# Gate columns and gate rows of an adaLN transformer block: from TensorE to GpSimd, VectorE and DRAM

## The chip, the cores and the metric

One NeuronCore of a Trainium2 chip runs the whole kernel. The metric is the device time of one execution in microseconds, as a median of runs. The engines are called by the names of the profile: PE (TensorE matmuls), PEld (TensorE weight loads), DVE (VectorE), ACT (ScalarE), POOL (GpSimd) and SP (SyncE, whose queue issues most of the DMAs).

## The reference

The block has 2048 rows of D = 1024, 32 query heads of 128, 4 key/value heads, the last 512 cached positions, and an FFN of width 3584. All inputs and the output are bf16.

```python
mod = (_silu(c) @ w_mod).reshape(c.shape[0], 6, 1, -1)
sa, ca, ga, sb, cb, gb = (mod[:, 0].copy(), ..., mod[:, 5].copy())
h = _layernorm(x, axis=-1) * (1 + ca) + sa
x = x + ga * _A_ref(h, A_k_cache, A_v_cache, A_wq, A_wo)   # attention, with wo
h = _layernorm(x, axis=-1) * (1 + cb) + sb
x = x + gb * _B_ref(h, B_w_gate, B_w_up, B_w_down)         # silu(h wg) * (h wu), then wd
```

c has one row, so the six modulation vectors sa to gb are the same for all 2048 rows of x. The two gates, ga and gb, scale the outputs of the attention and of the FFN.

## The kernel before

The rows of x are worked in four chunks of 512. For the attention the program is one loop over i from 1 to 129, with i = 32 * chunk + head. Each pass emits, in this order, the query projection for head i + 3 (8 matmuls of 512 columns into PSUM bank QB, emptied by a DVE cast at L640), the scores of head i - 1 (4 matmuls of 512 columns, whose exps ACT takes at L757 in two pieces of two banks), the product with V for head i - 2 (16 matmuls of 129 columns, normalised by DVE with a reciprocal at L775 and a multiply at L778), and a DMA transpose of that head's output into `oT_all` (L781, SP's queue). In passes up to 8 the query projection runs in every second pass only. When the last head of a chunk is through, `oproj` multiplies the 32 heads by wo, 8 pieces of 32 matmuls, and `resid` (L797 and L799) multiplies each piece by a gate row and adds it to x. After the attention, each chunk runs 28 gate and up column blocks and then the down projection, which ends in the same `resid`.

All instructions are issued in program order on each engine. `T.op` (L55) sets a semaphore wait ahead of an instruction for each buffer that another stream still writes or reads, so an instruction that waits holds everything behind it on its engine or, for a DMA, on SP's queue.

Small work is put into the passes by hand. `bg` is a list of generators; `run_bg(1)` at the end of each pass lets the first of them take one step. `ln_task` is one of these: for each of four 128-row tiles one step of `bn_stats` (L415), one of `bn_stats` and `bn_aggr` with two POOL instructions for the reciprocal deviation (L420, L422), and one of the norm (L426) with a DMA transpose (L445); three empty steps and four steps of two `modulate` (L431) follow.

The modulation vectors come in three ways. sa and ca are made before the loop by matmuls with one moving column. The last three vectors (sb, cb, gb) are made one column at a time from transposed weights by a DVE operation with an accumulator (`mod_col`, L585), in passes 38 to 89; for this, `sc_row` holds silu(c) along the free dimension in all partitions. The attention gate ga is made in passes 7 and 9 to 12, by 64 matmuls that take 128x128 blocks of `wga` as weights and one column of `sc_bf` (silu(c), one column for each 128 rows of w_mod) as the moving operand:

```python
for k in {7: (0, 1, 2, 3), 9: (4,), 10: (5,), 11: (6,), 12: (7,)}.get(i, ()):
    mod_mm(wga[:, k, :], B_wga[k], k, GCOLS)
```

The result is a vector across partitions (`mod_bf[:, NE:NF]`). `resid` and `mod_col` need such vectors as rows that are equal in all partitions. `row_task` does this three times (silu(c) into `sc_row`, ga into `rowb[0]`, gb into `rowb[1]`): POOL multiplies the identity by each of 8 columns (`diag`, L600), TensorE multiplies an all-ones matrix by the 8 diagonals (128 moving columns each, into bank XB), and DVE casts two halves to bf16 (L608).

The region `OFF_OT` of the arena holds early weights first and `oT_all`, 1 KB for each head, from then on. `wga` lies where the wo slots 6 and 7 come in passes 20 and 23.

Of the kernel before, what the change touches and what calls it, by code (L numbers as in the profile page):

```python
# [130 lines left out]
def bass_adaLN_cond__sliding_block_cached__swiglu_ffn__prompt_kernel(  # L131
# [50 lines left out]
    c_row = S_("c_row", [DT, P], BF16)  # L182
    sc_bf = S_("sc_bf", [P, DT], BF16)
    mod_bf = S_("mod_bf", [P, NJ], BF16)
    c6 = S_("c6", [P, DT], F32)
    mcol = S_("mcol", [P, 3 * DT], F32)
    gain = [S_("gain%d" % i, [P, DT], BF16) for i in range(2)]
    gain_f = S_("gain_f", [P, DT], F32)
    nmean = S_("nmean", [P, 1], F32)
# [19 lines left out]


    OFF_H20 = 154 * KB
    B_ident = _Buf("ident"); B_ones = _Buf("ones"); B_zw = _Buf("zw")
    B_diag = [_Buf("diag%d" % i) for i in range(4)]
    ident = arena.at(OFF_H20, [P], BF16, [B_ident])
    ones_bf = arena.at(OFF_H20 + 256, [P], BF16, [B_ones])
    diag = [arena.at(OFF_H20 + 512 + 256 * i, [P], BF16, [B_diag[i]]) for i in range(4)]
    zwarm = arena.at(OFF_H20 + 2048, [512], BF16, [B_zw])

    def bank(b, n=512, off=0):
        return ps[:, b * 512 + off:b * 512 + off + n]  # L220
# [7 lines left out]
    def psap(off, dims):  # L228
        return bass.AP(tensor=ps_t, offset=off, ap=[[4096, P]] + dims)
# [1 line left out]
    PB = [_Buf("bank%d" % b) for b in range(8)]  # L231
    B_x = [_Buf("x%d" % t) for t in range(ST)]
    B_mh = _Buf("mhalf")
    B_cT = _Buf("cT"); B_sc = _Buf("sc"); B_late = [_Buf("late%d" % i) for i in range(4)]; B_c6 = _Buf("c6"); B_mcol = _Buf("mcol"); B_scr = _Buf("scr")
    B_mode = _Buf("mode"); B_modc = _Buf("modc"); B_bq = _Buf("bq"); B_gf = _Buf("gf")
    B_nm = _Buf("nmean"); B_acc = _Buf("acc"); B_acc0 = _Buf("acc0")
    B_g = [_Buf("g%d" % i) for i in range(2)]
# [20 lines left out]
    with nc.Block() as block:  # L258

        @block.gpsimd  # L260
        def _(g):
# [5 lines left out]
            def mm(out_ap, lhsT, rhs, start, stop, reads, bank_buf, skip=False):  # L267
                T.op(PE, lambda: TE.matmul(out_ap, lhsT, rhs, start=start, stop=stop, skip_group_check=skip),  # L268
                     reads=reads, writes=[bank_buf])
# [15 lines left out]
            def finish(gen):  # L285
                while gen in bg:
                    run_bg(1)
# [3 lines left out]
            T.op(POOL, lambda: g.affine_select(out=ident, in_=ident, compare_op=ALU.not_equal,  # L291
                                               fill=1.0, base=0, pattern=[[-1, P]], channel_multiplier=1),
                 reads=[B_ident], writes=[B_ident])
            T.op(POOL, lambda: g.memset(ones_bf, 1.0), writes=[B_ones])
            T.op(POOL, lambda: g.memset(mhalf[:, :], -0.5), writes=[B_mh])
            T.op(POOL, lambda: g.memset(zwarm, 0.0), writes=[B_zw])

# [258 lines left out]

            B_wga = [_Buf("wga%d" % k) for k in range(DT)]
            wga = arena.at(OFF_WO + 48 * KB, [DT, D], BF16, B_wga)
            GCOLS = [(j, j) for j in range(DT)]

            def load_wga(i):
                T.op(dq("q_wga%d" % i), lambda: SP.dma_start(
                    wga[:, i * HK:(i + 1) * HK, :],
# [27 lines left out]
                     reads=[B_mcol], writes=[cbuf])  # L591


            def row_task(dst, dbuf, src, sbuf):
                T.op(POOL, lambda: g.tensor_copy(c6[:, :], src), reads=[sbuf], writes=[B_c6])

                def diags(n):
                    for q in range(4):
                        col = 4 * n + q
                        T.op(POOL, lambda: g.tensor_scalar(diag[q], ident, c6[:, col:col + 1], None, op0=ALU.mult),  # L600
                             reads=[B_ident, B_c6], writes=[B_diag[q]])

                diags(0)
                yield
                for n in range(2):
                    for q in range(4):
                        mm(bank(XB, P, q * P), ones_bf, diag[q], q == 0, q == 3, [B_ones, B_diag[q]], PB[XB], skip=True)
                    T.op(DVE, lambda: V.tensor_copy(dst[:, n * 512:(n + 1) * 512], bank(XB)),  # L608
                         writes=[PB[XB], dbuf])
                    if n == 0:  # L610
                        diags(1)
                    yield


            LEAD = 3
            NQT = 5; NEX = 2; NOS = 4
# [129 lines left out]
            o_s = [arena.at(OFF_OS + i * 1 * KB, [TPC, P], BF16, [B_os[i]]) for i in range(NOS)]  # L746
            oT_all = arena.at(OFF_OT, [Hq, CH], BF16, B_oT)

            def scores(i):
                ch, h = divmod(i, Hq)  # L750
                gk = h // rep
                qs = q_slot(i)
                es = i % NEX
                for kt in range(KT):
                    mm(bank(SCB + kt), kT_sb[:, gk * KT + kt, :], qT_s[qs], True, True, [B_kT[gk], B_qT[qs]], PB[SCB + kt])
                for kp in range(KT // 2):
                    T.op(ACT, lambda: A.activation(ex_s[es][:, 2 * kp:2 * kp + 2, :], banks2(SCB + 2 * kp), AF.Exp, scale=att_scale),  # L757
                         writes=[PB[SCB + 2 * kp], PB[SCB + 2 * kp + 1], B_ex[es]])
# [69 lines left out]
            def add_ln2(ch):  # L828
                s = ch % 2
                if ch == 0:  # L830
                    finish(rows)
                    h2s[0] = arena.at(OFF_H20, [DT, CH], BF16, B_h2[0])
                ln2[ch] = ln_task(ch, h2s[s], B_h2[s], 1, 3 * DT, B_late[1])
                bg.append(ln2[ch])

            LOADX = {19: 2, 40: 3}
            LOADT = {Hq + 2 + (9 * n) // 4: n for n in range(NL)}
            LOADO = {5 + (21 * p) // 8: p for p in range(8)}
            for i in range(1, NA + 2):
                ch, h = divmod(i, Hq)  # L840
                if i % 4 == 1 and i > 5 or i == 4:
                    load_wq((i + 4) // 4 + 1)
                if 2 <= i < NQ0:
                    q_shifted(i)
                if i in (2, 3):
                    load_wga(i - 2)
                if i in LOADX:
                    load_x(LOADX[i])
                if i in LOADO:
                    load_wo(LOADO[i])  # L850
                for gk in {2: (1,), 3: (2,), 4: (3,)}.get(i, ()):
                    k_turn(gk, XB)
                    kd, ks = k_evac(gk, XB)
                    T.op(DVE, lambda: V.tensor_copy(kd, ks), writes=[PB[XB], B_kT[gk]])
                    if gk == Hkv - 1:
                        for b_ in B_hT[1]:
                            for kb in B_kn:
                                b_.absorb(kb)
                if i == 17:
                    bg.append(row_task(sc_row, B_scr, sc_bf[:, :], B_sc))  # L860
                if i == 5:
                    add_ln1(1)
                if h == 2 and 1 <= ch < NCH - 1:
                    add_ln1(ch + 1)
                if h == 2 and ch == NCH - 1:
                    add_ln2(0)
                if i + LEAD < NA:
                    if (i + LEAD) % Hq == 0:
                        finish(ln1[(i + LEAD) // Hq])
                    if i == 1:  # L870
                        scores(0)
                    if i in (1, 3, 5):
                        q_bias_mm(i + 1, i + 3, QB)
                    if i > NQ0:
                        qproj(i + LEAD)
                    elif i % 2 == 0:
                        qproj(NQ0 - 1 + i // 2)
                for k in {7: (0, 1, 2, 3), 9: (4,), 10: (5,), 11: (6,), 12: (7,)}.get(i, ()):
                    mod_mm(wga[:, k, :], B_wga[k], k, GCOLS)
                    if k == DT - 1:  # L880
                        T.op(DVE, lambda: V.tensor_copy(mod_bf[:, NE:NF], psap(XB * 512, [[2, DT]])), writes=[PB[XB], B_late[0]])
                        rows = row_task(rowb[0], B_row[0], mod_bf[:, NE:NF], B_late[0])
                        bg.insert(0, rows)
                if i - 4 in LOADT:
                    n = LOADT[i - 4]
                    mod_col(n)
                    g0, last = divmod(n, DT)
                    if last == DT - 1:
                        mod_take(g0, B_late[g0 + 1])
                        if g0 == 1:  # L890
                            mod_gain(1, B_late[2], B_g[1])
                        elif g0 == 2:
                            rows = row_task(rowb[1], B_row[1], mod_bf[:, 5 * DT:6 * DT], B_late[3])
                            bg.insert(0, rows)
                if i in LOADT:
                    load_mt(LOADT[i])
                n = i - (NA - LEAD)
                if 0 <= n <= 2:
                    oproj_mm(NCH - 1, 0, QB, 8 * n, 8 * n + 8)
                elif n >= 3:  # L900
                    oproj_mm(NCH - 1, 1, XB, 8 * (n - 3), 8 * (n - 3) + 8)
                if 1 <= i - 1 < NA:
                    scores(i - 1)
                if 0 <= i - 2 < NA:
                    pv(i - 2)
                    ch2, h2 = divmod(i - 2, Hq)
                    if h2 == Hq - 1 and ch2 < NCH - 1:
                        finish(rows)
                        oproj(ch2)
                run_bg(1)  # L910


            NWG = 3
# [146 lines left out]
```

## Time and profile before

| what | us |
|---|---|
| median of 3 runs | 1275.35 (1275.09 to 1275.66) |
| span of the profiled execution | 1273.8 |
| PE busy | 1267.0 |
| DVE busy | 479.6 |
| ACT busy | 341.5 |
| POOL busy | 42.0 |
| 256 exps at L757, each | 1.023 |
| 24 diagonal multiplies at L600, each | 0.616 |
| 24 `mod_col` at L585, each | 1.214 |

The page gives the profiled execution as the span from its first to its last instruction; the runs are timed from outside and stand 1.55 us above that. A row of the timeline gives the start in us from the span's start, the time taken, the engine, the line, the operation, its output and inputs with their shapes, how many instructions are merged into the row, and in brackets how long the engine had been idle and what it waited for. In a row of merged instructions, the time runs from the first start to the last end.

### The profile page before, as it was taken

To read this page: it belongs to the slowest core of one execution; us is meant where nothing else is said; L and a number is where in the kernel's file an instruction comes from. 1 tells how busy PE (TensorE), PEld (TensorE's weight loads), DVE (VectorE), ACT (ScalarE), POOL (GpSimd) and SP (SyncE) were. 2 spreads that over 40 slices of the span, in tenths; PEclk is the share of its full clock that TensorE was granted. 3 is DMA by queue.
4 is the path that set the end of the run, shared out by engine and by line. 5 is a ranking of instruction groups with operands and counts; after the bars stand their busy time and mean duration, and the time that the engine had idled before them with its cause. 6 is when DMAs were issued, how large, how long until landed. Compare 5 with 4: busy or idle time off the path is not lost.

```text
span 1273.8 us, 17943 instructions
## 1 busy us (share of the span) xinstructions
PE 1267.0 (99%) x7683; PEld 645.7 (51%) x7683; DVE 479.6 (38%) x897; ACT 341.5 (27%) x388; POOL 42.0 (3%) x102
## 2 busy tenths in 40 slices
PE   8999999999999999999999999999999999999999
PEld 5665545555455564455544444444444444444444
DVE  4655315764147652365322331233212331222222
ACT  4555304554025550155510111011100111011100
POOL 1020000000000010000000000000000000000000
PEclk9999999999999999999999999999999999999999
DMA  9999403876018641055253973056411644035200
GB/s 306 271 235 224 99 1 84 194 169 133 1 34 191 140 104 38 5 129 118 67 147 99 285 222 121 25 154 152 148 60 56 192 140 132 17 120 161 66 9 25
DMA packets 235854, 155.31 MB, mean 122 GB/s; under 512 B 129024, under 2 KB 222080, under 8 KB 235776
## 3 DMA queue, kind: packets, MB, share of 16 engines
q1 hardware_dynamic: 177520, 95.45, 30.7%
q10 hardware_dynamic: 58256, 58.73, 14.7%
q8 instruction: 60, 0.98, 0.3%
q14 instruction: 18, 0.15, 0.0%
HBM read 119.54 MB, written 4.19 MB: 97 GB/s over the span
## 4 chain that ended last, share of the span: by engine, by line
PE 99%; DMA 1%; DVE 0%; SPq 0%; ACT 0%; issue 0%
PE ps L268 98%; DMA arena<-in_A_wq_dram 1%; DVE arena L671 0%; SPq L331 0%; SPq L306 0%; PE ps L272 0%; ACT arena L757 0%; DVE arena L666 0%; DVE tmp L797 0%; DVE arena L799 0%; DVE bq L661 0%
## 5 line engine op out<-in xcount | busy, mean ns | idle before, releaser
L268 PE MATMUL ps<-arena 128*128 128x512 bf16 (+1 forms) x7378 | 1260.7, 334 | 4.0 <-POOL arena L408 2.2
L268 PEld LDWEIGHTS ps<-arena 128*128 128x128 bf16 x7378 | 635.6, 98 | 621.0 <-issue 3.9
L757 ACT ACTIVATE arena<-ps 128x1024 bf16<-128x1024 f32 x256 | 261.9, 1023 | 350.3 <-PE ps L268 338.4
L989 ACT ACTIVATE arena<-ps 128x512 bf16<-128x512 f32 x112 | 66.9, 597 | 506.4 <-PE ps L268 506.4
L990 DVE TENSOR_TENSOR arena<-ps,arena 128x512 bf16<-128x512 f32 x112 | 77.4, 691 | 276.6 <-PE ps L268 276.6
L797 DVE TENSOR_TENSOR tmp<-ps,rowb 128x512 f32<-128x512 f32 (+1 forms) x65 | 44.4, 683 | 318.8 <-PE ps L268 318.8
L640 DVE CAST arena<-ps 128x512 bf16<-128x512 f32 x120 | 82.9, 691 | 53.8 <-PE ps L268 53.8
L778 DVE TENSOR_TENSOR arena<-ps,rl 128x512 bf16<-128x512 f32 x128 | 88.5, 691 | 4.7 <-DVE rl L775 0.3
L775 DVE RECIPROCAL rl<-ps 128x4 f32<-128x4 f32 x128 | 23.3, 182 | 118.3 <-PE ps L268 118.3
L415 DVE BATCH_NORM_STATS2 st<-x_res 128x6 f32<-128x512 bf16 x62 | 42.3, 683 | 3.6 <-DMA x_res<-in_A_x_dram 3.5
L420 POOL TENSOR_SCALAR rstd<-mv 128x1 f32<-128x1 f32 x28 | 6.3, 226 | 888.2 <-DVE mv L419 888.2
L585 DVE SCALAR_TENSOR_TENSOR arena<-arena 128x1024 bf16<-128x1024 bf16 x24 | 29.1, 1214 | 0.0
L799 DVE TENSOR_TENSOR arena<-tmp,x_res 128x512 bf16<-128x512 f32 (+1 forms) x33 | 22.3, 675 | 1.1
L799 DVE TENSOR_TENSOR x_res<-tmp,x_res 128x512 bf16<-128x512 f32 x32 | 22.1, 692 | 1.1
L431 DVE TENSOR_SCALAR arena<-arena,gain,mod_bf 128x512 bf16<-128x512 bf16 x56 | 20.3, 404 | 0.0
L426 DVE TENSOR_SCALAR nsc<-x_res,mv,rstd 128x1024 bf16<-128x1024 bf16 x30 | 16.0, 533 | 0.0
L422 POOL TENSOR_TENSOR rstd<-rstd,mhalf 128x1 f32<-128x1 f32 x28 | 15.8, 564 | 2.3
L600 POOL TENSOR_SCALAR arena<-arena,c 128x128 bf16<-128x128 bf16 x24 | 14.4, 616 | 32.7 <-PE ps L268 32.4
L268 PEld LDWEIGHTS ps<-sc_bf,arena 128*128 128x128 bf16 x192 | 6.6, 96 | 2.3 <-DMA arena<-in_w_mod_dram 0.3
L268 PE MATMUL ps<-sc_bf,arena 128*128 128x1 bf16 x192 | 6.8, 163 | 0.0
L419 DVE BATCH_NORM_AGGREGATE mv<-st 128x2 f32<-128x12 f32 x28 | 5.8, 209 | 1.0
L653 DVE COPY arena<-ps 128x512 f32<-128x512 f32 x4 | 2.7, 688 | 8.3 <-PE ps L268 8.3
(53 smaller groups left out, 50.7 us busy)
## 6 DMA issues: line engine op xcount, KB each, us to landing
arena<-in_A_wq_dram SPq DMA_DIRECT2D x31, 1024.0 KB, 6.1
arena<-in_B_w_gate_dram ACTq DMA_DIRECT2D x28, 1024.0 KB, 5.4
arena<-in_B_w_up_dram ACTq DMA_DIRECT2D x28, 1024.0 KB, 8.1
arena<-in_A_wo_dram SPq DMA_DIRECT2D x8, 1024.0 KB, 6.4
arena<-in_B_w_down_dram SPq DMA_DIRECT2D x7, 1024.0 KB, 8.4
out_dram<-arena SPq DMA_DIRECT2D x15, 256.0 KB, 2.0
x_res<-in_A_x_dram SPq DMA_DIRECT2D x3, 1024.0 KB, 6.7
arena<-in_w_mod_dram SPq DMA_DIRECT2D x8, 256.0 KB, 6.3
```

The source lines that it names most:

```text
L268: T.op(PE, lambda: TE.matmul(out_ap, lhsT, rhs, start=start, stop=stop, skip_group_check=skip), reads=reads, writes=[bank_buf])
L415: T.op(DVE, lambda: V.bn_stats(st_[sl][:, hf * 6:hf * 6 + 6], x_res[:, t, hf * 512:hf * 512 + 512]), reads=[B_x[t]], writes=[B_st[sl]])
L431: T.op(DVE, lambda: V.tensor_scalar(dst[:, dt, :], dst[:, dt, :], gain[gi][:, dt:dt + 1], mod_bf[:, ccol + dt:ccol + dt + 1], op0=ALU.mult ...
L585: T.op(DVE, lambda: V.scalar_tensor_tensor(mt[n % 2], mt[n % 2], 1.0, sc_row, op0=ALU.mult, op1=ALU.mult, accum_out=mcol[:, n:n + 1]), rea ...
L640: T.op(DVE, lambda: V.tensor_copy(qT_s[qs], bank(b)), writes=[PB[b], B_qT[qs]])
L757: T.op(ACT, lambda: A.activation(ex_s[es][:, 2 * kp:2 * kp + 2, :], banks2(SCB + 2 * kp), AF.Exp, scale=att_scale), writes=[PB[SCB + 2 * k ...
L775: T.op(DVE, lambda: V.reciprocal(rl[r][:, :].rearrange("p (a b) -> p a b", a=2), psap(PVB * 512 + P, [[512, 2], [130, 2]])), writes=both + ...
L778: T.op(DVE, lambda: V.tensor_tensor(o_s[os_].rearrange("p (a b) d -> p a b d", a=2), psap(PVB * 512, [[512, 2], [130, 2], [1, P]]), rlb, A ...
L797: T.op(DVE, lambda: V.tensor_tensor(tmp[s][:, 0:n], bank(b, n), rowb[ri][:, c0:c0 + n], ALU.mult), reads=[B_row[ri]], writes=[PB[b], B_tmp ...
L799: T.op(DVE, lambda: V.tensor_tensor(dst[:, c0:c0 + n], tmp[s][:, 0:n], x_res[:, t, c0:c0 + n], ALU.add), reads=[B_tmp[s], B_x[t]], writes= ...
L989: T.op(ACT, lambda: A.activation(sg_s[ss], bank(gb), AF.Silu), writes=[PB[gb], B_sg[ss]])
L990: T.op(DVE, lambda: V.tensor_tensor(guT[:, ft, :], bank(ub), sg_s[ss], ALU.mult), reads=[B_sg[ss]], writes=[PB[ub], B_gu[ft]])
```

## The change

ga is no longer made by TensorE. `wga` now serves as it lies in memory, with the rows of w_mod across partitions. For each of the 8 groups of 128 rows, a group is multiplied by its column of `sc_bf` (one scalar for each partition) and summed into an fp32 accumulator `g_acc` of 128x1024: groups 0 to 3 by POOL in pieces of 512 columns (`gate_part`, passes 4 to 13), groups 4 to 7 by DVE in one instruction each (`gate_row`, passes 16 to 19). Then POOL splits `g_acc` into a bf16 part and the bf16 remainder (`gate_split`), two DMA transposes on SP's queue turn the parts (`gate_turn`, passes 23 and 24), and DVE sums each of them over the former partitions and adds the two sums (`gate_sum`, passes 26 and 27).

The three rows are no longer made by `row_task`. `row_put` writes a vector from across the partitions to a row in DRAM, and `row_get` reads that row back into all 128 partitions, both on SP's queue.

The new tiles lie in `OFF_OT` in the place of heads that are written later in the first chunk: `g_tmp` at heads 16 and 17, `g_part` at 24 to 27, `g_acc` and after it `g_turn` at 28 to 31.

```diff
-            T.op(POOL, lambda: g.memset(ones_bf, 1.0), writes=[B_ones])
...
-            def row_task(dst, dbuf, src, sbuf):
...
+            def row_put(r, src, sbuf):
+                T.op(Q_dr[r], lambda: SP.dma_start(d_rows[r:r + 1, :].rearrange("o (k p) -> p (o k)", p=P), src, allow_slow_non_contiguous=True),
+                     reads=[sbuf], writes=[B_dr[r]])
+
+            def row_get(r, dst, dbuf):
+                rep_ap = bass.AP(tensor=d_rows.tensor, offset=r * D, ap=[[0, P], [1, D]])
+                T.op(Q_rw[r], lambda: SP.dma_start(dst, rep_ap), reads=[B_dr[r]], writes=[dbuf])
...
+            def gate_part(n):
+                k, hf = divmod(n, 2)
+                a = g_acc[:, hf * 512:(hf + 1) * 512]
+                w = wga[:, k, hf * 512:(hf + 1) * 512]
+                if k == 0:
+                    T.op(POOL, lambda: g.tensor_scalar(a, w, sc_bf[:, k:k + 1], None, op0=ALU.mult),
+                         reads=[B_wga[k], B_sc], writes=[B_ga[hf]])
+                else:
+                    T.op(POOL, lambda: g.tensor_scalar(g_tmp, w, sc_bf[:, k:k + 1], None, op0=ALU.mult),
+                         reads=[B_wga[k], B_sc], writes=[B_gx])
+                    T.op(POOL, lambda: g.tensor_tensor(a, a, g_tmp, ALU.add), reads=[B_gx], writes=[B_ga[hf]])
...
+            def gate_row(k):
+                T.op(DVE, lambda: V.scalar_tensor_tensor(g_acc, wga[:, k, :], sc_bf[:, k:k + 1], g_acc, op0=ALU.mult, op1=ALU.add),
+                     reads=[B_wga[k], B_sc], writes=B_ga)
+
+            def gate_split():
+                T.op(POOL, lambda: g.tensor_copy(g_part[0], g_acc), reads=B_ga, writes=[B_gp[0]])
+                T.op(POOL, lambda: g.tensor_tensor(g_part[1], g_acc, g_part[0], ALU.subtract),
+                     reads=B_ga + [B_gp[0]], writes=[B_gp[1]])
+
+            def gate_turn(i):
...
+                T.op(Q_gt[i], lambda: SP.dma_start_transpose(g_turn[i], g_part[i]), reads=[B_gp[i]], writes=[B_gt[i]])
...
+            def gate_sum(i):
+                T.op(DVE, lambda: V.tensor_reduce(gsum[:, i * DT:(i + 1) * DT], g_turn[i], mybir.AxisListType.X, ALU.add),
+                     reads=[B_gt[i]], writes=[B_gsum])
+                if i == 1:
+                    T.op(DVE, lambda: V.tensor_tensor(gcol[:, :], gsum[:, 0:DT], gsum[:, DT:2 * DT], ALU.add),
+                         reads=[B_gsum], writes=[B_gcol])
...
+            GATEP = {4: (0, 1), 5: (2,), 7: (3,), 8: (4,), 10: (5,), 11: (6,), 13: (7,)}
+            GATER = {16 + n: NGP + n for n in range(DT - NGP)}
+            GATET = {23: 0, 24: 1}
+            GATES = {26: 0, 27: 1}
+            t2 = Hq + 6 + (9 * (NL - 1)) // 4
+            PUTT = {22: (0, sc_bf[:, :], B_sc), 29: (1, gcol[:, :], B_gcol), t2 + 2: (2, mod_bf[:, 5 * DT:6 * DT], B_late[3])}
+            GETT = {25: (0, sc_row, B_scr), 31: (1, rowb[0][:, :], B_row[0]), t2 + 4: (2, rowb[1][:, :], B_row[1])}
...
-                if i == 17:
-                    bg.append(row_task(sc_row, B_scr, sc_bf[:, :], B_sc))
+                if i in GATET:
+                    gate_turn(GATET[i])
+                if i in GATES:
+                    gate_sum(GATES[i])
+                if i in GATER:
+                    gate_row(GATER[i])
+                if i in PUTT:
+                    row_put(*PUTT[i])
+                if i in GETT:
+                    row_get(*GETT[i])
...
-                for k in {7: (0, 1, 2, 3), 9: (4,), 10: (5,), 11: (6,), 12: (7,)}.get(i, ()):
-                    mod_mm(wga[:, k, :], B_wga[k], k, GCOLS)
-                    if k == DT - 1:
-                        T.op(DVE, lambda: V.tensor_copy(mod_bf[:, NE:NF], psap(XB * 512, [[2, DT]])), writes=[PB[XB], B_late[0]])
-                        rows = row_task(rowb[0], B_row[0], mod_bf[:, NE:NF], B_late[0])
-                        bg.insert(0, rows)
...
                 run_bg(1)
+                for n in GATEP.get(i, ()):
+                    gate_part(n)
+                if i == max(GATER):
+                    gate_split()
```

NGP is 4, DT is 8, NL is 24, so t2 is 89. The code before and after these lines stays as it is.

More of the change, by code (lines that the diff above doesn't have):

```diff
@@ L184, in bass_adaLN_cond__sliding_block_cached__swiglu_ffn__prompt_kernel @@
     mod_bf = S_("mod_bf", [P, NJ], BF16)
-    c6 = S_("c6", [P, DT], F32)
     mcol = S_("mcol", [P, 3 * DT], F32)
+    gsum = S_("gsum", [P, 2 * DT], F32)
+    gcol = S_("gcol", [P, DT], BF16)
     gain = [S_("gain%d" % i, [P, DT], BF16) for i in range(2)]
@@ L211, in bass_adaLN_cond__sliding_block_cached__swiglu_ffn__prompt_kernel @@
     OFF_H20 = 154 * KB
-    B_ident = _Buf("ident"); B_ones = _Buf("ones"); B_zw = _Buf("zw")
-    B_diag = [_Buf("diag%d" % i) for i in range(4)]
+    B_ident = _Buf("ident"); B_zw = _Buf("zw")
+    B_gcol = _Buf("gcol")
+    B_dr = [_Buf("dr%d" % i) for i in range(3)]
     ident = arena.at(OFF_H20, [P], BF16, [B_ident])
-    ones_bf = arena.at(OFF_H20 + 256, [P], BF16, [B_ones])
-    diag = [arena.at(OFF_H20 + 512 + 256 * i, [P], BF16, [B_diag[i]]) for i in range(4)]
+    d_rows = nc.dram_tensor("mod_rows", [3, D], BF16, kind="Internal").ap()
     zwarm = arena.at(OFF_H20 + 2048, [512], BF16, [B_zw])
@@ L233, in bass_adaLN_cond__sliding_block_cached__swiglu_ffn__prompt_kernel @@
     B_mh = _Buf("mhalf")
-    B_cT = _Buf("cT"); B_sc = _Buf("sc"); B_late = [_Buf("late%d" % i) for i in range(4)]; B_c6 = _Buf("c6"); B_mcol = _Buf("mcol"); B_scr = _Buf("scr")
+    B_cT = _Buf("cT"); B_sc = _Buf("sc"); B_late = [_Buf("late%d" % i) for i in range(4)]; B_gsum = _Buf("gsum"); B_mcol = _Buf("mcol"); B_scr = _Buf("scr")
     B_mode = _Buf("mode"); B_modc = _Buf("modc"); B_bq = _Buf("bq"); B_gf = _Buf("gf")
@@ L558, in _ @@
             wga = arena.at(OFF_WO + 48 * KB, [DT, D], BF16, B_wga)
-            GCOLS = [(j, j) for j in range(DT)]
             def load_wga(i):
@@ L591, in mod_take @@
                      reads=[B_mcol], writes=[cbuf])
-            def row_task(dst, dbuf, src, sbuf):
[L595 to L612, printed above, removed]
+            Q_dr = [dq("q_dr%d" % i) for i in range(3)]
+            Q_rw = [dq("q_rw%d" % i) for i in range(3)]
+            Q_gt = [dq("q_gt%d" % i) for i in range(2)]
+            def row_put(r, src, sbuf):
[4 more added lines that the diff above has]
+                T.op(Q_rw[r], lambda: SP.dma_start(dst, rep_ap), reads=[B_dr[r]], writes=[dbuf])
             LEAD = 3
@@ L747, in _ @@
             oT_all = arena.at(OFF_OT, [Hq, CH], BF16, B_oT)
+            NGP = 4
+            B_ga = [_Buf("ga%d" % i) for i in range(2)]
+            B_gx = _Buf("gx")
+            B_gp = [_Buf("gp%d" % i) for i in range(2)]
+            B_gt = [_Buf("gt%d" % i) for i in range(2)]
+            g_acc = arena.at(OFF_OT + 28 * KB, [D], F32, B_ga)
+            g_tmp = arena.at(OFF_OT + 16 * KB, [512], F32, [B_gx])
+            g_part = [arena.at(OFF_OT + (24 + 2 * i) * KB, [D], BF16, [B_gp[i]]) for i in range(2)]
@@ new lines, in _ @@
+            g_turn = [arena.at(OFF_OT + (28 + 2 * i) * KB, [DT, P], BF16, [B_gt[i]]) for i in range(2)]
+            def gate_part(n):
[9 more added lines that the diff above has]
+                    T.op(POOL, lambda: g.tensor_tensor(a, a, g_tmp, ALU.add), reads=[B_gx], writes=[B_ga[hf]])
+                if n == 2 * NGP - 1:
+                    for h in (16, 17):
+                        B_oT[h].absorb(B_gx)
@@ new lines, in gate_turn @@
+            def gate_turn(i):
+                for b_ in B_ga:
+                    B_gt[i].absorb(b_)
+                T.op(Q_gt[i], lambda: SP.dma_start_transpose(g_turn[i], g_part[i]), reads=[B_gp[i]], writes=[B_gt[i]])
+                for h in (24 + 2 * i, 25 + 2 * i):
+                    B_oT[h].absorb(B_gp[i])
+            def gate_sum(i):
[4 more added lines that the diff above has]
+                         reads=[B_gsum], writes=[B_gcol])
+                    for h in range(28, Hq):
+                        for b_ in B_gt:
+                            B_oT[h].absorb(b_)
@@ L830, in add_ln2 @@
                 if ch == 0:
-                    finish(rows)
                     h2s[0] = arena.at(OFF_H20, [DT, CH], BF16, B_h2[0])
@@ L891, in _ @@
                             mod_gain(1, B_late[2], B_g[1])
-                        elif g0 == 2:
-                            rows = row_task(rowb[1], B_row[1], mod_bf[:, 5 * DT:6 * DT], B_late[3])
-                            bg.insert(0, rows)
                 if i in LOADT:
@@ L907, in _ @@
                     if h2 == Hq - 1 and ch2 < NCH - 1:
-                        finish(rows)
                         oproj(ch2)
                 run_bg(1)
+                for n in GATEP.get(i, ()):
+                    gate_part(n)
+                if i == max(GATER):
+                    gate_split()
             NWG = 3
```

## The prediction

> **What bounds the kernel now.** I read the page's busy shares and the chain that ended last, then the granted clock, then the DVE timeline as a ruler of the attention loop.
>
> ```profile
> PE 1267.0 (99%) x7683; PEld 645.7 (51%) x7683; DVE 479.6 (38%) x897; ACT 341.5 (27%) x388; POOL 42.0 (3%) x102
> PEclk9999999999999999999999999999999999999999
> PE 99%; DMA 1%; DVE 0%; SPq 0%; ACT 0%; issue 0%
> ```
>
> TensorE is busy for 1267.0 of 1273.8 us, at the full clock (mean 1.000), and the chain is TensorE work. So a matmul taken out is worth its own time, and any other engine costs something only where it makes TensorE wait. The ruler is the reciprocal on L775, once in each loop pass, 0.20 us after the last pv matmul of the pass:
>
> ```profile
> 53.96 0.18 DVE L775 RECIPROCAL rl<-ps 128x4 f32<-128x4 f32 x1 [1.08 <-PE ps L268]
> 57.66 0.18 DVE L775 RECIPROCAL rl<-ps 128x4 f32<-128x4 f32 x1 [1.28 <-PE ps L268]
> ...
> 68.75 0.18 DVE L775 RECIPROCAL rl<-ps 128x4 f32<-128x4 f32 x1 [1.21 <-PE ps L268]
> 72.24 0.18 DVE L775 RECIPROCAL rl<-ps 128x4 f32<-128x4 f32 x1 [1.08 <-PE ps L268]
> 75.96 0.18 DVE L775 RECIPROCAL rl<-ps 128x4 f32<-128x4 f32 x1 [1.08 <-PE ps L268]
> ```
>
> 72.24 less 68.75 is the bare pass (3.497 with more digits; 35.87 belongs to pass i=2, so 53.96 to i=8, 72.24 to i=13). A pass with 8 gate-column matmuls takes 3.70 (57.66 less 53.96), one with 4 row matmuls 3.72 (75.96 less 72.24).
>
> **What is taken from TensorE.** Passes 9 to 12 lose 8 gate matmuls each: 4 x 0.20 = 0.80 us. The three row tasks lose two groups of four 128-column matmuls each: 6 x 0.224 = 1.34 us. The 32 gate matmuls of pass 7 are another matter, because ACT is late there:
>
> ```profile
> 47.69 0.94 PE L268 MATMUL ps<-sc_bf,arena 128*128 128x1 bf16 x32
> ...
> 48.50 1.70 PE L268 MATMUL ps<-arena 128*128 128x512 bf16 x16
> ...
> 48.74 1.33 PEld L268 LDWEIGHTS ps<-arena 128*128 128x128 bf16 x15 [0.15 <-ACT arena L757]
> ```
>
> Without them the scores start at 47.69 instead of 48.50. But their third matmul needs PSUM that the running pair of exps (46.55, 2.14 long) frees at 48.69; it then starts at 48.74 instead of 48.93 (48.50 + 2 x 0.2155). I count 0.17 us, the floor, rather than 0.81, the ceiling, because TensorE already meets ACT there. Sum: 0.80 + 1.34 + 0.17 = 2.31 us.
>
> The removed DVE casts (6 of 0.68 us), the diagonals on POOL and the memset of the ones save nothing: no TensorE wait names them, and the start waits for the c row (PEld 0.84 us behind its DMA).
>
> **GpSimd's half.** Two pieces of one instruction, six of two, on 128x512. The one-operand multiply is not in the trace at this size. Below it stands the 128x512 memset (0.52 us), above it four times the 128x128 multiply (4 x 0.616 = 2.46); by the slope from a 128x1 (0.226) to a 128x128 it is 0.226 + 511 x 0.00307 = 1.80, which I take, being the same operation. The fp32 add has only a 128x1 power (0.56) as a row: 0.56 to 3.6 (twice the multiply), taken at 1.8. The weights land by 29.4 + 7.8 = 37.2 us. Pieces 0 to 2 (four instructions, 7.2 us) end at 44.4; the layernorm step behind them on POOL gets its input at 49.65. Pieces 3 and 4 (7.2) run from 50.7 to 57.9; the next step is due at 59.5. Pieces 5 and 6 run from 60.4 to 67.6, due about 69. If the add costs 3.6, pieces 3 and 4 end at 61.5 and the rstd is 0.8 us late for the norm, which DVE's slack below covers.
>
> DVE and GpSimd may also hold each other up. The trace has one meeting of a GpSimd run with a fast DVE operation:
>
> ```profile
> 72.44 2.34 POOL L600 TENSOR_SCALAR arena<-arena,c 128x128 bf16<-128x128 bf16 x4 [2.15 <-PE ps L268]
> ...
> 93.15 2.61 POOL L600 TENSOR_SCALAR arena<-arena,c 128x128 bf16<-128x128 bf16 x4
> ...
> 94.50 0.54 DVE L426 TENSOR_SCALAR nsc<-x_res,mv,rstd 128x1024 bf16<-128x1024 bf16 x1
> ```
>
> GpSimd's four took 0.27 us more than where DVE read PSUM; the norm took its usual 0.54 and began on time. So DVE won, at no cost. The operations exposed are two shifts (passes 4 and 5), three norms (7, 10, 13) and the first modulates against the split. From above, each is held for a whole 1.8 us instruction; a norm may slip about 1.25 us before TensorE notices (0.37 idle ahead of the cast, 0.9 between cast and the next use of its bank), so three norms cost up to 3 x 0.55 = 1.6 us. The lower end is nothing; a gain is excluded, since no instruction gets shorter by company. I take 0.2, near the row.
>
> The Trainium skill, SBUF — State Buffer, section "Who interferes with whom", speaks against this change: the port pair that the two engines share is an exclusive lock, held for a whole instruction, and whoever starts second is fully blocked. By it DVE would lose whenever GpSimd is first; the one meeting in this trace does not show that, and it alone decides my 0.2. By the rule the sum would end near 1.6 worse.
>
> **DVE's half.** Four gate_row operations, passes 16 to 19, each ahead of the cast that empties the q projection's bank. Nearest row: L585, the same form on 128x1024, 1.214 us, its successor 1.14 behind its start; fp32 operands are not in the trace, from 0.69 (512 fp32 columns) to 2.4 (twice it), taken at 1.21. Pass 16 is the tight one, as its gate_row follows bn_stats and bn_aggr:
>
> ```profile
> 79.69 0.18 DVE L775 RECIPROCAL rl<-ps 128x4 f32<-128x4 f32 x1 [1.08 <-PE ps L268]
> ...
> 81.23 0.21 DVE L419 BATCH_NORM_AGGREGATE mv<-st 128x2 f32<-128x12 f32 x1
> 81.41 0.69 DVE L640 CAST arena<-ps 128x512 bf16<-128x512 f32 x1
> 83.18 0.18 DVE L775 RECIPROCAL rl<-ps 128x4 f32<-128x4 f32 x1 [1.08 <-PE ps L268]
> ```
>
> The cast moves from 81.41 to 82.55 and ends at 83.24, seen by TensorE at 83.29 (0.05 of latency, as behind the exp); it wants the bank at 82.98. Loss 0.31 us (nothing at 0.69, 1.5 at 2.4). Behind a norm (pass 17) the cast ends 0.16 before its bank is due, behind nothing earlier still: no loss in 17 to 19. The two reductions (passes 26, 27; no row, taken as 1.21 too) follow empty steps, likewise free.
>
> **SP's queue.** Two transposes like the layernorm's (issue 1.26, landing 3.6, at most 7.7). The first is issued at 106.9, behind the last wo load, and is needed at 115.5 (pass 26); the second at 109.8, needed at 119.0. At worst both are 0.9 us early. The split feeding them starts at 92.2 and takes 3.6 to 11, so it is done by 103. The wo load of pass 20 now waits for gate_row, done at 92.2; SP reaches it at 98.3. Each of the six row DMAs costs an issue of about 0.53; SP has over 0.4 us spare in each pass.
>
> The puts are the open point: each writes 1,024 runs of 2 bytes to DRAM, which no row shows. A wq load is also 1,024 runs:
>
> ```profile
> arena<-in_A_wq_dram SPq DMA_DIRECT2D x31, 1024.0 KB, 6.1
> ...
> out_dram<-arena SPq DMA_DIRECT2D x1, 128.0 KB, 1.7
> ```
>
> Between 1.6 (the 64 KB output) and 11.3 us (the slowest wq load), I take 6, being nearest in runs. The gate's put leaves at 128 behind a wq load and its get stands in SP's queue at 134.8; the get waits, and behind it the transposes of heads 29 to 31, but TensorE needs those (and the row) only at about 150. Counting back the get's issue, three transposes and 2.9 of landing (7.5 us together), the put may take 14.4 us before TensorE waits. For pass 22's put the room to its get is 11 us, and more behind it. The third row is first read in the down projection, after 645 us. Cost 0, also at 11.3.
>
> The Trainium skill, VectorE: DVE Perf Modes, section "The three transpose paths", warns that a strided plain copy is 19 times slower than a DMA transpose. By its 1.309 us for 128x128, a put of a sixteenth as many elements would be about 1.6 us (an estimate): this too stays covered.
>
> **Sum.** -2.31 + 0.31 + 0.2 = -1.8 us. The profiled span of 1273.8 becomes 1272.0; the median of the runs, 1275.35, lies 1.55 above the span, which I carry over: 1273.5 us. A measurement of this kernel tells about 0.2%, 2.55 us, from no change, so the forecast lies inside that band.
>
> **Rivals.**
> - Faster, 1272.4: pass 7 returns its full 0.81 and neither 0.31 nor 0.2 is lost (-2.95). For it: DVE is only 38% busy. Against it: the ACT wait at 48.74 and the back-to-back DVE at 81.4.
> - Slower, the put: it decides above 14.4 us, and from there each us of landing is one us of time. At 19.3 us it eats 2.3 and 2.55 more; at 25 it gives 1275.35 - 1.8 + 10.6 = 1284. For it: 2-byte runs are far from any row, and DMA is over 90% busy to 127 us. Against it: 256-byte transposes land in 2.9 us.
> - DVE held by GpSimd, or GpSimd slower than 2.6 us an instruction (10.5 us from 50.7 to the rstd's last useful start, for four), so that norms wait for rstd: three norms 1.6, a modulate behind a long split up to 3 more, 1275 to 1278. For it: GpSimd is busy through most of passes 4 to 14. Against it: the meeting at 94.5.
> - The change does nothing for TensorE: excluded by the ruler for all but pass 7.
>
> **How the numbers follow.** Forecast 0.57, faster 0.14, the put 0.12, DVE held 0.17. Two thirds of the last end beyond the band, so slower is 0.12 + 0.11 = 0.23, the same 0.57 + 0.06 = 0.63, faster 0.14. The range runs from 1272.2 (the faster rival with rounding) to 1278.0 (the top of the held case); it leaves out the put and little else. The forecast's own range is 1272.4 to 1275.0.
>
> **What would show it.** Right: passes 9 to 15 and the three former row passes at 3.497; pass 7 only 0.1 to 0.2 shorter; one pass near 16 about 0.3 longer; no SP wait on a put beyond a few us. Wrong: TensorE waits that name L640's bank in passes 5 to 14 (DVE held), a late first oproj near 143 us (the put), reductions waiting for the transposes, or GpSimd instructions well over 2.6 us.

## The result: 2.3% slower, and the profile after

The changed kernel takes 1304.84 us (median of 5 runs, 1302.57 to 1307.3) against 1275.66 for the kernel before beside it (5 runs): a ratio of 1.0228, 95% interval 1.0217 to 1.0239. The forecast was 1273.5, so it was missed by about 31 us. The profiled execution took 1305.02 us, its span is 1303.1, 29.3 more than before.

The head of the page after, the clock by slices, and the chain that ended last:

```profile
span 1303.1 us, 17621 instructions
...
PE 1263.0 (97%) x7454; PEld 644.0 (49%) x7595; DVE 485.1 (37%) x897; ACT 341.7 (26%) x388; POOL 51.0 (4%) x90
...
PEclk9998889999999999999999999999999999999999
...
PE 92%; DMA 5%; DVE 1%; issue 1%; SPq 1%; ACT 0%
```

TensorE has 88 matmuls fewer, the 64 of the gate columns and the 24 of the rows, as the count of its weight loads shows (7595 for 7683; the trace lacks some records of matmuls, so their own count says less). But its share fell from 99 to 97% and the clock dips in three slices, from 98 to 195 us. DMA, 1% of the chain before, now has 5%. The ruler (the reciprocal, now on L815) says where. Each row gives what the passes took beyond the same passes of before:

| stretch | more or less, us |
| --- | --- |
| to the first ruler tick (pass 2) | -0.28 |
| passes 3 to 15 | -1.41 |
| pass 17, whose bank is freed by pass 16's cast, behind a gate_row | +0.36 |
| passes 26 (18.269 for 3.496) and 27 (6.626 for 3.496) | +17.90 |
| passes 29, 30: row matmuls gone | -0.45 |
| passes 32, 33 and the first output projection | +10.30 |
| second output projection | +0.8 |
| passes 91, 92: row matmuls gone | -0.45 |
| pass 94 | +2.39 |

The three large stalls sum to 30.6 us, and each follows one put of a row (the write of `row_put` to DRAM; a get is the read of `row_get`). SP's timeline shows the first:

```profile
103.43 0.58 SPq L597 DMA_DIRECT2D mod_rows<-sc_bf  x1
...
106.88 0.58 SPq L831 DMA_DIRECT2D arena<-in_A_wo_dram  x1
107.50 7.46 SPq L775 DMA_TRANSPOSE arena<-arena  x1
115.00 10.44 SPq L821 DMA_TRANSPOSE arena<-arena  x1
125.48 3.63 SPq L775 DMA_TRANSPOSE arena<-arena  x1
```

The put (L597) is issued at 103.43. The first turn of the gate (L775) then holds SP's queue for 7.46 us, the next output transpose (L821) for 10.44, where the ones at 100.27, 104.06 and 129.15 took 3.11, 2.77 and 1.27. In the trace's packet records the put's 1,024 packets leave between 106.9 and 107.3, at 9 ns each; the landing comes only at 123.0. So the time lies behind the sending. Windows of five microseconds show what the rest of the core does (columns: busy time of PE, PEld, DVE, ACT, POOL, then the granted clock, DMA share and GB/s):

```profile
100.00:105.00 5.00, 5.00 (x36) 2.77 (x35) 3.54 (x9) 2.19 (x4) 0.00 (x0) 1.00 1.21 254
...
110.00:115.00 5.00, 4.95 (x36) 2.77 (x35) 2.26 (x5) 2.68 (x3) 0.00 (x0) 1.00 0.48 21
115.00:120.00 5.00, 1.78 (x21) 1.19 (x18) 0.00 (x0) 2.05 (x2) 0.00 (x0) 1.00 0.73 18
120.00:125.00 5.00, 0.00 (x0) 0.00 (x0) 0.00 (x0) 0.00 (x0) 0.00 (x0) 0.53 0.72 73
...
130.00:135.00 5.00, 3.27 (x8) 1.19 (x9) 3.75 (x6) 0.00 (x0) 0.00 (x0) 0.50 0.89 249
```

From 110 to 120 the core's DMA moves 18 to 21 GB/s; the kernel before moves 226 to 259 in the same ten microseconds. Then TensorE stops, and when it starts again its clock is at 0.50. DVE's timeline, and behind it TensorE's, tell who waits for whom:

```profile
113.32 0.18 DVE L815 RECIPROCAL rl<-ps 128x4 f32<-128x4 f32 x1 [1.08 <-PE ps L269]
113.54 0.69 DVE L818 TENSOR_TENSOR arena<-ps,rl 128x512 bf16<-128x512 f32 x1
129.86 1.22 DVE L780 TENSOR_REDUCE gsum<-arena 128x8 f32<-128x1024 bf16 x1 [15.63 <-DMA arena<-arena]
131.00 0.68 DVE L629 CAST arena<-ps 128x512 bf16<-128x512 f32 x1
```

```profile
112.78 4.00 PE L269 MATMUL ps<-arena 128*128 128x129 bf16 x33
131.73 8.61 PE L269 MATMUL ps<-arena 128*128 128x512 bf16 x37 [14.95 <-DVE arena L629]
```

The reduction waits 15.63 us for the turn, which landed 22.3 us after its issue. The cast of the q projection stands behind the reduction on DVE, and TensorE waits 14.95 us for the bank which that cast frees. Restarted at half the clock, it loses 3.13 us more in pass 27.

The second put is seen among SP's waits, where the get waits for it:

```profile
SPq L602 <- DMA mod_rows<-gcol: 11.1, 1, 11.1
SPq L602 <- DMA mod_rows<-mod_bf: 4.4, 1, 4.4
```

It is issued at 144.51 and its get at 161.91, 17.4 us later; the third takes 13.9 (482.30 to 496.25). Behind the second get stand the last heads' transposes, for which TensorE waits 4.2 us in the first output projection; from 170 to 180 us its clock is then 0.65 and 0.66 on average.

### The profile page after: what moved, and what is told of

Its sections match the earlier page's. It is cut to its first block, busy times and chain, and to the rows that moved or that the text cites. A ratio compares the mean times of both kernels' runs of the same rounds, so it can differ in the third digit from the quotient of the medians.

```text
span 1303.1 us, 17621 instructions
## 1 busy us (share of the span) xinstructions
PE 1263.0 (97%) x7454; PEld 644.0 (49%) x7595; DVE 485.1 (37%) x897; ACT 341.7 (26%) x388; POOL 51.0 (4%) x90
## 3 DMA queue, kind: packets, MB, share of 16 engines
q10 hardware_dynamic: 58256, 58.73, 14.3%
## 4 chain that ended last, share of the span: by engine, by line
PE 92%; DMA 5%; DVE 1%; issue 1%; SPq 1%; ACT 0%
PE ps L269 92%; DMA arena<-arena 3%; DMA arena<-in_A_wq_dram 2%; DVE arena L629 0%; DVE arena L818 0%; ACT arena L797 0%; DVE arena L660 0%; SPq L331 0%; SPq L306 0%; SPq L821 0%; DVE arena L764 0%; PE ps L273 0%; DVE arena L583 0%; DVE rl L815 0%; DVE arena L655 0%
## 5 line engine op out<-in xcount | busy, mean ns | idle before, releaser
L797 ACT ACTIVATE arena<-ps 128x1024 bf16<-128x1024 f32 x256 | 262.1, 1024 | 379.5 <-PE ps L269 367.7
L815 DVE RECIPROCAL rl<-ps 128x4 f32<-128x4 f32 x128 | 23.3, 182 | 113.1 <-PE ps L269 112.8
L839 DVE TENSOR_TENSOR arena<-tmp,x_res 128x512 bf16<-128x512 f32 (+1 forms) x33 | 22.3, 676 | 1.1
L756 POOL TENSOR_SCALAR arena<-arena,sc_bf 128x512 f32<-128x512 bf16 x6 | 9.5, 1583 | 0.2
L780 DVE TENSOR_REDUCE gsum<-arena 128x8 f32<-128x1024 bf16 x2 | 2.4, 1213 | 15.6 <-DMA arena<-arena 15.6
L758 POOL TENSOR_TENSOR arena<-arena 128x512 f32<-128x512 f32 x6 | 7.6, 1266 | 0.5
```

The lines of the kernel that those rows point to most:

```text
L815: T.op(DVE, lambda: V.reciprocal(rl[r][:, :].rearrange("p (a b) -> p a b", a=2), psap(PVB * 512 + P, [[512, 2], [130, 2]])), writes=both + ...
L839: T.op(DVE, lambda: V.tensor_tensor(dst[:, c0:c0 + n], tmp[s][:, 0:n], x_res[:, t, c0:c0 + n], ALU.add), reads=[B_tmp[s], B_x[t]], writes= ...
```

## The experiments

The cuts of code show the lines that matter; `...` stands for lines left out, and long lines are shortened.

**Part by part.** Theory A: the puts, each of 1,024 runs of two bytes into DRAM, land late and slow every other transfer meanwhile. Rival B: the gate's own steps do it, GpSimd's hold on DVE or the two turns that DVE waits for. The first kernel keeps the gate part and gives the three rows back to the diagonal matmuls:

```diff
-                if i in PUTT:
-                    row_put(*PUTT[i])
-                if i in GETT:
-                    row_get(*GETT[i])
+                if i == 17:
+                    bg.append(row_task(sc_row, B_scr, sc_bf[:, :], B_sc))
+                if i == 27:
+                    rows = row_task(rowb[0], B_row[0], gcol[:, :], B_gcol)
+                    bg.insert(0, rows)
```

> Half of the change: the gate columns by GpSimd and VectorE, split, two transposes, two sums; the three rows again by diagonals and TensorE. Theory A (the three puts of 1,024 runs of 2 bytes jam the DMA path, and that is the whole loss): the time is that of before, less 0.97 us (gate matmuls: 0.80 + 0.17), plus 0.36 (the pass behind gate_row), so about 1275.0 us; both transposes land within 8 us and VectorE does not wait for them. Theory B (the two extra transposes, or GpSimd's work beside VectorE, cost the 15.6 us wait of VectorE): 1290 us or more, the wait at the first reduction stays.

Measured 1275.71 us, ratio 1.0003 (0.9993 to 1.0012). The two turns, issued near 106 and 110, land without DVE waiting (first the issues, then the landings):

```profile
L801 SPq DMA_TRANSPOSE arena<-arena x2: 1247/1712/2176, 105.9 to 109.8; - x2
...
DMA to landing us min/median/max: 5.7/6.3/6.8
```

B falls: none of the large stalls is there. The gate part has small prices of its own, which eat what it saves: by the ruler 0.96 us gained in passes 7 to 12, and 0.36 lost behind gate_row, 0.22 in pass 28 and 0.29 at the second output projection. The time is 0.7 above what A gave. The other half, the gate by matmul as before and the rows by put and get:

```diff
-            GATET = {23: 0, 24: 1}
-            GATES = {26: 0, 27: 1}
...
-  29: (1, gcol[:, :], B_gcol)
+  29: (1, mod_bf[:, NE:NF], B_late[0])
...
+                    mod_mm(wga[:, k, :], B_wga[k], k, GCOLS)
```

> The other half: gate columns by TensorE as before, the three rows by put and get through DRAM in the same passes (22/25, 29/31, 91/93). Theory A: each put lands 12 to 20 us after its issue; the second costs about 10 us at the first output projection, the third about 2.4, the first some us where the output transposes are held; less 1.34 for the row matmuls: 1286 to 1292 us. Theory B: 1274 us, that is 1.3 us less than before.

Measured 1298.38 us, ratio 1.0182 (1.0167 to 1.0197): A's direction, but a loss above its bounds. With no reduction in DVE's order, the first put still costs 9.0 us (passes 27 to 29), the second 8.6, the third 4.1. What waits now is the normalisation of the heads' outputs, for a slot that an output transpose frees, and SP waits for a put as in the changed kernel:

```profile
DVE arena L770 <- DMA arena<-arena: 12.1, 4, 7.0
...
SPq L605 <- DMA mod_rows<-mod_bf: 10.9, 1, 10.9
```

**The runs' width alone.** Rival C: not the narrow runs, but any way through DRAM costs this. The changed kernel, with one thing altered: the row's columns are permuted, so that each partition's eight values lie together and the put writes 128 runs of 16 bytes. The rows then hold their values in another order, and the output with them.

```diff
-  d_rows[r:r + 1, :].rearrange("o (k p) -> p (o k)", p=P)
+  d_rows[r:r + 1, :].rearrange("o (p k) -> p (o k)", p=P)
```

> The whole change, but each put writes 128 runs of 16 bytes in place of 1,024 runs of 2 bytes (each partition's eight values stay together, so the rows come back with their columns in another order, and the result is not the reference's). Theory A, priced by the run (about 12 us for 1,024, so 12 ns each): a put lands after about 2 + 1.5 = 3.5 us, no wait is left, about 1273.6 us. Rival C (a write to DRAM that is read back has a fixed price of 12 us or more, whatever its runs): landings of 12 us and more, 1290 to 1305 us.

Measured 1274.79 us, ratio 0.9996 (0.9986 to 1.0005). The same bytes on the same queue at the same places now land like this (last column: us from issue to landing):

```profile
mod_rows<-sc_bf SPq DMA_DIRECT2D x1, 2.0 KB, 4.6
mod_rows<-gcol SPq DMA_DIRECT2D x1, 2.0 KB, 6.1
mod_rows<-mod_bf SPq DMA_DIRECT2D x1, 2.0 KB, 1.6
```

No get waits and the ruler has none of the three stalls. C falls, and this one line of the kernel is the whole loss.

**What sets a put's price.** Each of the three kernels here ran once. First, before's kernel with six puts, each waiting for the one ahead, beside the weight loads of the last MLP chunk:

```diff
+                if jf == (NCH - 1) * FT + 1:
+                    probes()
```

> The kernel before, with six puts added on SP's queue in the last chunk's gate and up blocks, where SP has nothing else to do, each waiting for the one ahead: 8 runs of 256 bytes; 128 of 16; 512 of 2; 1,024 of 2; 1,024 of 4; 1,024 of 2 that lie 64 bytes apart. Theory A, a price for each run: about 2, 3.5, 8, 14, 14 and 14 us to landing. Variant A2, a price for runs that fall on the same 64-byte piece of memory: 2, 3, 8, 14, 8 to 14 and about 3. Rival C, a fixed price: six alike. The kernel's time should stay near 1275.5 us unless the weight loads on ACT's queue are jammed beyond their lead of two groups.

SP's timeline: each put leaves when the one ahead has landed, so differences of starts are prices (the third, fourth and fifth put, then the sixth, which landed 5.7 after its issue).

```profile
1135.35 0.37 SPq L1036 DMA_DIRECT2D d<-sc_bf  x1
1151.14 0.37 SPq L1038 DMA_DIRECT2D d<-sc_bf  x1
1174.39 0.36 SPq L1040 DMA_DIRECT2D d<-gain_f  x1
1188.76 0.36 SPq L1043 DMA_DIRECT2D d<-sc_bf  x1
```

512 runs of two bytes take 15.8 us, 1,024 take 23.25, 1,024 of four bytes 14.4; ahead of them 8 runs of 256 bytes took 3.0 and 128 of 16 bytes 5.1. The sixth put has as many runs as the fourth, equally short, and differs in where they land. The number of runs is not the price. From 1135 to 1151 us, while the 512 runs landed, the core's DMA moved 19 GB/s; in the kernel before it moves 139 there. The time was missed: 1284.33 us where about 1275.5 stood, because TensorE came to wait for weights on another queue (they are issued by ACT):

```profile
PE ps L268 <- DMA arena<-in_B_w_up_dram: 5.7, 1, 5.7
```

To leave out the load, four puts in the first output projection, where little else is in flight (the core's DMA moves 109 GB/s up to 150 us, at most 33 after that):

```diff
+                    if ch == 0 and k == 2:
+                        probes()
```

> The kernel before, with four puts of 1,024 or 512 runs of 2 bytes on SP's queue during the first output projection, when no other DMA runs; each waits for the one ahead. In this order: runs 64 bytes apart; runs 16 bytes apart; 512 runs side by side (1 KB); 1,024 side by side (2 KB). Theory A (a price for each run): 14, 14, 8 and 14 us to landing. Theory A2 (a price for runs that share a 64-byte piece of memory): about 4, 5 to 8, 8 and 14. Were it the other DMA traffic that made the puts slow in the earlier run, all four would land within 4 us. The kernel's time stays near 1275.5 us as long as the four together stay under about 45 us.

```profile
144.85 0.58 SPq L833 DMA_DIRECT2D e<-sc_bf  x1
149.13 0.37 SPq L835 DMA_DIRECT2D e<-sc_bf  x1
153.31 0.36 SPq L837 DMA_DIRECT2D e<-sc_bf  x1
167.65 0.36 SPq L839 DMA_DIRECT2D e<-sc_bf  x1
```

4.3 us at 64 bytes apart, 4.2 at 16, 14.3 for 512 dense runs; the last, 1,024 dense, landed 15.6 after its issue. Idle neighbours do not make a dense put cheap (1275.25 us in all, since nothing waited). Three more fill the gap: 8 and 4 bytes apart, and 256 dense runs, in the same place.

> The kernel before with three more puts of 2-byte runs in the first output projection, each behind the one ahead: 1,024 runs 8 bytes apart; 1,024 runs 4 bytes apart; 256 runs side by side (512 bytes). The earlier probes took 4.3 us at 64 bytes apart, 4.2 at 16, 14.3 for 512 side by side and 15.6 for 1,024. Theory A2 (what counts is how many runs fall on one 64-byte piece; 32 of them cost about 12 us, so 0.4 each): 8 on a piece give about 6, 16 about 9, and 256 side by side, still 32 on a piece, about 14. Theory A (a price for each run, hidden by something in the earlier probe): 256 runs give about 5 us and the two others 14 to 15.

```profile
SPq L836 <- DMA e<-sc_bf: 12.2, 1, 12.2
SPq L834 <- DMA e<-sc_bf: 5.7, 1, 5.7
```

These are SP's waits for the 4-byte and the 8-byte spacing, which took 12.6 and 6.3 us from issue to issue; the 256 dense runs landed in 16.5. (Its 1277.25 us holds 1.6 that were there at the first ruler tick, ahead of the probes.) Counted by how many runs fall on the same 64 bytes of DRAM, the prices are 4.3 us for 1, 4.2 for 4, 6.3 for 8, 12.6 for 16, and 16.5, 14.3 and 15.6 for 32, whether 256, 512 or 1,024 runs are sent. So with little traffic beside them density sets the price, not the count; beside the weight loads 512 dense runs took 15.8 and 1,024 took 23.25. The size of the target alone is not it either: 128 runs of 16 bytes fill the same 2 KB as 1,024 dense ones and landed in 1.6 to 6.1 us. That 64 bytes is the size of the piece, whether it matters that dense neighbours come from different partitions, and what the memory does there, no run shows.

**Who pays.** D1: the transfers behind the put on SP's queue. D2: all transfers of the core. The three puts are moved to ACT's queue:

```diff
-            Q_dr = [dq("q_dr%d" % i) for i in range(3)]
+            Q_dr = [dq("q_dr%d" % i, A) for i in range(3)]
...
-                T.op(Q_dr[r], lambda: SP.dma_start(
+                T.op(Q_dr[r], lambda: A.dma_start(
```

> The whole change, with the three puts issued on ACT's queue in place of SP's; everything else as it was. Theory D1 (what stands behind a put waits because one queue is worked in order): the transposes and loads on SP's queue no longer stand behind the put, VectorE's 15.6 us wait goes, and what is left is the get's own wait on SP: under 1290 us. Theory D2 (while the puts drain, the DMA engines or the memory serve every queue slowly): the wait at the first reduction stays above 8 us, and the time stays within 8 us of 1305.

Measured 1301.6 us, ratio 1.0206 (1.0187 to 1.0224); the first put lands 20.5 us after its issue. The reduction waits less, and TensorE waits for wq loads on SP's queue instead:

```profile
DVE gsum L780 <- DMA arena<-arena: 4.4, 1, 4.4
...
PE ps L269 <- DMA arena<-in_A_wq_dram: 10.9, 3, 6.6
```

The time is D2's; the reduction's wait is below what D2 gave and above nothing, so the split between the queues fits neither fully. With the w_up wait of the probe above, where the load was on ACT's queue and the puts on SP's, the jam is seen across queues both ways.

Then the turns ahead of the put, and its get after the last transpose, so that nothing that DVE needs by the gate stands behind it:

```diff
-            GATET = {23: 0, 24: 1}
+            GATET = {21: 0, 22: 1}
...
-            GETT = {25: (0, sc_row, B_scr),
+            GETT = {34: (0, sc_row, B_scr),
```

> The whole change, with the gate's two transposes issued in passes 21 and 22, ahead of the first put, in place of 23 and 24, and the first get in pass 34 in place of 25. Theory A: the transposes land before the put drains, VectorE's 15.6 us wait goes; the second and third put still cost some 10 and 2 us and the first still slows the output transposes: 1288 to 1296 us. Theory B (the transposes themselves, or the reductions, are slow): the wait stays, 1300 us or more.

Measured 1303.35 us, ratio 1.0219 (1.0201 to 1.0238): a miss, nothing was won. The reduction's wait is gone and another has its place, the normalisation that waits for an output transpose:

```profile
DVE arena L818 <- DMA arena<-arena: 14.3, 2, 9.5
```

The first put still costs about 16 us (passes 27 to 29: 12.431, 6.795 and 7.712). The loss isn't the gate's: it goes to whichever transfer is needed next.

**The change with wide runs.** A version that keeps what the change takes from TensorE: the silu of the c row is computed by ACT from the row form, the two late vectors are written as columns of a 128x128 tile that one DMA transpose turns, and every put is 8 runs of 256 bytes. The gate_row step goes behind the cast.

```diff
+  T.op(ACT, lambda: A.activation(s8[0:DT, :], c_row[:, :], AF.Silu), ...)
+  def pad_turn(i):
+      T.op(Q_pt[i], lambda: SP.dma_start_transpose(padt..., pad), ...)
-  d_rows[r:r + 1, :].rearrange("o (k p) -> p (o k)", p=P), src
+  d_rows[r:r + 1, :].rearrange("o (k p) -> (o k) p", p=P), src
```

> A version meant to keep what the change saves: silu(c) is taken once more from the c row as it lies (8 partitions of 128) by ACT; the two gate vectors are turned by one DMA transpose of a 128x128 tile; so each put writes 8 runs of 256 bytes. And gate_row stands behind the cast of its pass in place of ahead of it. Theory A: puts land in about 3 us, nothing waits for them; less 2.31 us for the removed matmuls, no 0.36 at pass 16; up to 0.8 for the wait at the second output projection that the run with 16-byte runs showed: 1273.0 to 1274.0 us. Rival C: puts of 12 us and more, 1290 us and more.

Measured 1274.65 us, ratio 0.9995 (0.9986 to 1.0004). The 0.36 at pass 17 is gone. From pass 2 to pass 92 the ruler gains 1.67 us, in which 0.63 is lost at the second output projection (59.385 for 58.750): the savings are 2.30. Another 0.56 goes behind the last tick, 0.41 of it in a wait for an output transpose in the last output projection. Two guesses on these: E1, small tiles that moved the addresses of the large ones; E2, something else. The same version with the old addresses kept (the small tiles now behind the arena):

> The version with wide runs, with the new small tiles allocated behind the arena, so that every tile of the kernel before lies at its old address (the change had moved the arena by 48 bytes). Theory E1 (the 0.6 us at the second output projection and some 0.4 at the last one come from the moved addresses, which make the DMA transposes land later): both go, about 1273.4 us. Theory E2 (they come from the new DMAs' and the passes' timing): as the version with wide runs, about 1274.6.

Measured 1274.63 us, ratio 0.9993 (0.9984 to 1.0002). The second output projection is still 0.79 longer, and TensorE's timeline there has a wait for an output transpose that before's lacks:

```profile
315.30 4.92 PE L273 MATMUL ps<-arena 128*128 128x512 bf16 x21 [0.61 <-DMA arena<-arena]
```

And the kernel before with 48 unused bytes ahead of the arena:

```diff
+    shift_pad = S_("shift_pad", [P, 12], F32)
```

> The kernel before with 48 unused bytes ahead of the arena, nothing else. Theory E1: the pass behind the second output projection is 0.3 to 0.7 us longer, 1275.8 to 1276.5 us in all. Theory E2: no change, 1275.5 us.

Measured 1275.47 us, ratio 1.0002 (0.9993 to 1.0011). E1 falls. Why TensorE comes to wait there for an output transpose, so that this stretch is 0.5 to 0.8 us longer in every version with both halves of the change, stays open. The half with the gate part alone shows 0.29 of it, the half with the puts alone nothing. No version is faster by more than the measurement can tell.

## Why the prediction was wrong

**What failed: the price of a put and who pays it.** The step reads "I take 6, being nearest in runs", between 1.6 and 11.3, and "Cost 0". Measured landings: 19.6, 17.4 and 13.9 us, all above the upper bound. The choice of row was the error: a wq load has 1,024 runs too, but not 32 of two bytes on the same 64 bytes of DRAM. The probes show that the count does not set the price (1,024 runs land in 4.3 us when 64 bytes apart). No row of the trace had that pattern, and the bound should have been left open above. Two of the prediction's own signs of being wrong are in the profile: reductions that wait for the transposes, and a late first output projection.

The second half was worse. The put's cost was counted as the wait of those who read the row. For the first put the text found 11 us of room to its get "and more behind it", and indeed that get never held TensorE. What held it was a turn issued 4 us after the put, and, with the turn out of the way, an output transpose. The turns were priced at 3.6 us, "at most 7.7"; by themselves they land in 5.7 and 6.8, behind the put the first took 22.3.

**The rival "the put"** had the right cause, at 0.12, and a price per microsecond that was far too small: above 14.4 us each us of landing was to cost one, so 17.4 would have cost 3.0. (Its 19.3 us for leaving the band counts a gain of 2.3, where the sum had 1.8; by the sum it is 18.75.) The second put cost 10.3: the last heads' transposes and wq loads were late in themselves, and TensorE then ran for some microseconds at a lower clock.

**What held.** The terms taken from TensorE: 2.31 by the sum, 2.30 measured where nothing covers them. Passes 9 to 12 and the former row passes went to 3.497, and pass 7 to 2.407 for 2.570, so the floor of 0.17 was right and the ceiling of 0.81 was not. The gate_row loss was 0.36 where 0.31 stood. The reductions took 1.22 for 1.21, which is luck, as no row stood behind that figure. GpSimd's multiply took 1.58 and its add 1.26, both taken at 1.8.

**Held by GpSimd: cost near, reason half right.** The meeting at 94.5 was read as "DVE won", and the sum took 0.2. After the change three norms meet GpSimd: one starts inside a multiply, two start 0.05 us ahead of an add. GpSimd's timeline and DVE's:

```profile
50.44 1.59 POOL L756 TENSOR_SCALAR arena<-arena,sc_bf 128x512 f32<-128x512 bf16 x1
...
59.72 1.58 POOL L756 TENSOR_SCALAR arena<-arena,sc_bf 128x512 f32<-128x512 bf16 x1
61.39 1.26 POOL L758 TENSOR_TENSOR arena<-arena 128x512 f32<-128x512 f32 x1
```

```profile
50.85 0.56 DVE L426 TENSOR_SCALAR nsc<-x_res,mv,rstd 128x1024 bf16<-128x1024 bf16 x1
...
61.34 1.60 DVE L426 TENSOR_SCALAR nsc<-x_res,mv,rstd 128x1024 bf16<-128x1024 bf16 x1
62.85 0.68 DVE L629 CAST arena<-ps 128x512 bf16<-128x512 f32 x1
```

The norm takes 0.54 us by itself. Inside the multiply it took 0.56, and the multiply was no longer than the others. Beside the add it took 1.60 and ended 0.29 after the add; the one at 71.83, beside another add, took 1.60 too. The runs with the gate part alone, with 16-byte runs and with wide runs show the same 0.56 and 1.60. So the reading holds beside a multiply, as at 94.5, and fails beside an add. The pass stays at 3.497 all the same, because 1.06 is less than the 1.25 of slack that the prediction counted; nothing was lost where 0.2 stood. The Trainium skill, SBUF — State Buffer, section "Who interferes with whom", says that the shared port pair is an exclusive lock for a whole instruction. The two norms beside an add agree with a lock, though by the start times they came first; the norm at 50.85 does not, as the multiply had begun 0.41 us before it.

The other rule weighed there, VectorE: DVE Perf Modes, "The three transpose paths", gave an estimate of 1.6 us for a put by its factor of 19. The trace does not agree: 13.9 to 19.6.

## What to carry to other kernels

A row that goes from one value per partition to DRAM should be turned first, or permuted, so that each run is 16 bytes or more: the same 2 KB landed in 1.6 to 6.1 us with runs of 16 bytes, and in 3.0 with runs of 256, instead of 13.9 to 19.6. Price a DMA whose pattern the trace does not have by where its runs land, leave its upper bound open, and ask of every transfer issued in the 20 us behind it, on every queue, who needs it next; moving the wait of one only hands it to the next. Here the change takes 2.3 us from TensorE, and the cheapest of its three puts cost 2.4.

## What the runs showed of the hardware

Dense two-byte writes to DRAM slow the core's other transfers, to 18 to 21 GB/s for ten microseconds, on other queues as well, although their own packets are sent within 0.4 to 1.5 us. A put of 256 dense runs costs as much as one of 1,024.

After a stop TensorE pays twice. Its last matmul ahead of the stall ended at 116.8; the clock was 1.00 up to 120 and 0.53 on average from 120 to 125, so it fell near 120.3, and after the restart at 131.7 it was back near 137.4 (0.76 on average from 135 to 140). The Trainium skill, TensorE: Matmul & The Clock Gate, "Part 1: The HAM clock gate (the "warmup" mystery)", gives an idle window of about 3.4 us for the fall; the 3.5 of this stall agrees. The stall in the first output projection does not: its last matmul ended at 169.53, and the 0.65 on average from 170 to 175 puts the fall near 171.5, 2.0 us later, behind two shorter stops of 1.53 and 2.02.
